# Fixed orders of the first part drawn anew on all engines, with a narrower product for the low part of v

## The chip, the cores and the metric

The kernel runs on one core of a Trainium2 chip, in one launch. The metric is device microseconds (us) of one execution, on that core; the time of a kernel is the median of its timed runs. Besides these runs there is one profiled execution, whose trace gives the start and the length of every instruction. The engines are called as in the profile: PE (matrix products), PEld (loading of the stationary operand for PE), DVE, ACT and POOL (three engines for element-wise work) and SP (which issues the transfers, DMA).

## What is computed

The reference is a block of a transformer on one sequence of 2048 tokens with 576 features, all in float32:

```python
mod = (silu(c) @ w_mod).reshape(1, 6, 1, 576)          # sa, ca, ga, sb, cb, gb
h = layernorm(x) * (1 + ca) + sa
q, k, v = split(h @ wqkv)                              # 32 heads of 18 features
pq, pk = phi(q), phi(k)                                # phi(t) = t + 1 if t > 0 else exp(t), + 1e-6
kv = einsum("bhsd,bhse->bhde", pk, v)                  # state sums, over all tokens
z  = einsum("bhsd->bhd", pk)
o  = einsum("bhqd,bhde->bhqe", pq, kv) / (einsum("bhqd,bhd->bhq", pq, z) + 1e-6)
x = x + ga * (o @ wo)
h = layernorm(x) * (1 + cb) + sb
x = x + gb * (silu(h @ w1) @ w2)                       # 576 -> 4608 -> 576
```

## The kernel before

**Numbers in two parts.** Products on PE are not taken in plain float32 but in a rounded form ("fp32r" in the profile). Each operand is split into a high part (the rounded value) and a low part (the rest, a subtraction on DVE or POOL, line 121). A product of two such operands is three matmuls on PE: high by high, high by low and low by high. Low by low is left out as too small to matter. `x_passes` (L222 to L226) records these three passes for most products of the first part.

**Stages.** The first part, some 370 us, computes attention token tile by token tile (16 tiles of 128 tokens). The modulation vectors are summed from `w_mod`, which is transferred in pieces (`raw`) and multiplied and added on DVE into `tmod` (`mod_piece`, L519). The same is done at the very start for the two vectors that the first layer norm needs (L360, L362, tile `hT`). For a group of tiles at a time, x is normalised (`layernorm`, L160 to L193, tile `xt`, in two forms: 576 columns, and a copy of the last 64), transposed on PE (L214) and multiplied with `wqkv` (L226, banks `psK`). `kv_mm` (L582 to L592) adds each tile's state sums: for each of five groups of heads it keeps a 128 by 128 piece of v stationary, once its high part (h = 0) and once its low part (h = 1), and moves the matching columns of k, 128 columns of the high part and 128 of the low part, 256 in all. So low by low is computed here, though it isn't needed: the bank `kvp` holds two halves of 128 columns for a group, which are added afterwards. These are 16 x 5 x 2 = 160 matmuls of 256 columns.

When the sums are complete, they are multiplied with `wo`, which turns the attention of a token into one product with a matrix `mpart`. Then each tile goes through `attn_step` (L1193): POOL multiplies q by z (`prod`, L1195), DVE sums it and takes the reciprocal (`q_norm`, L744 to L756), POOL multiplies q by it (`pn`, L752) and copies the last 64 columns once more (L754), PE transposes `pn` in five pieces of 128 columns (`q_transpose`, L811; only the fifth needs the copy), ACT and DVE split the result into high and low part (`qT`), and PE multiplies it with `mpart` (`attn_out`, L817). In between stand the layer norm and the transposes for the MLP (`xn`, `H`, `S`, `hT`) and the first products of the MLP, for the first group of its hidden columns: `mlp_up` (L885) and `down` (L896), whose results DVE adds to the accumulators (L901).

**The rest.** From about 370 us on, the MLP goes by units. A unit takes 256 of the hidden columns and half of the tokens, and computes the first product (`up`, L1323) and the second (`down`, L1396) by a scheme with seven products for two by two blocks instead of eight; the sums of blocks that the scheme needs are made ahead (L1136 to L1139), and the results are added on DVE (L1404). Two banks take the `down` products in turn, so a bank must be added up before PE may begin the next one in it. The names of the seven operands of the second product are ha, hb, hc, hd, he with a half (0 or 1).

**What sets the order.** From the third unit on, the order is that of the program text, on all engines (`manual_schedule`, L1554). For all that is ahead of it, tables of fixed numbers set the order (`ORDERS`, L55 to L105): `arrange` (L107 to L117) takes the instructions of an engine as a scheduler has laid them down and ties each to the one that the table puts before it, by a dependency that costs no wait on a semaphore. The tables have a row for each engine. DVE, ACT and POOL do their instructions strictly in this order: one that waits holds up all behind it.

Of the kernel before, what the change touches and what calls it, by code (L numbers as in the profile page):

```python
# [16 lines left out]
P = 128  # L17
# [5 lines left out]
def kernel(ctx: ExitStack, tc, A_x, A_wqkv, A_wo, B_x, B_w1, B_w2, c, w_mod, out):  # L23
# [28 lines left out]
    def f32(ap):  # L52
# [4 lines left out]
            0-105 114 106-108 115 109-113 116-2585  # L57
        """,
        "DVE": """
            2-3 1 0 4 6-7 11-12 8 5 13-14 18 15 9 16 10 17 19-24 29 25 28 26-27 30-31 43-44 33-34 36-37 35 38 32 39  # L60
            41 40 45 42 47 46 50 48-49 62-63 51 64 52 65-66 57 87 67 58 53 59 56 84-85 60 80 86 88 55 83 81 68-69 82
            70-72 122 73 54 74 61 89 75-76 123 78-79 91 77 90 92 124 93-94 96-97 125 98 126 100 127 99 95 103 101
            104-105 102 108 106-107 109-111 132-133 135 134 136 138-139 137 141-142 140 143-144 112-113 146-147 145
            114 148 117 115 149 118 116 119-121 128 131 129-130 150-151 224 222-223 225-226 152-154 157 155 158 156
            159 162 176 160-161 177-179 163 180 165 228 164 181 227 166-167 169-170 168 171-173 193-194 196 195 197
            199 198 200 202 201 203-205 174 206 175 207 182 185 209 183 208 186 188 187 210 184 189 192 190 211 191
            212-213 216 214 217 215 218 220 219 221 229-230 232-233 231 234-237 240 238-239 241-243 246 244 247 245
            248-249 252 250-251 253-255 258 256-257 259 262 260-261 263 266 268 267 270 269 271 264-265 272-273
            275-277 281 274 279 282 280 278 283-285 288 286 289 303 295-296 290 306 302 307 291 314 292 315 297 323
            298-299 293 308 300 324 294 304 331 309-310 287 311 301 312 305 332 316 340 313 317-321 341 325 322 351  # L70
            326-329 333 352 362 334-336 330 337 363 343-344 338 370 345-346 339 347 349 342 348 371 380 350 353-361
            381 398 364-369 372 399 416 373-375 377 376 378 417 424 385 382 384 379 387-388 391-392 394 425 402 386
            389 403 390 404-406 393 407 413 383 408 397 395 409-411 396 414 418 415 412 419-422 400-401 423 426-428
            432 429 431 430 435 433-434 437-440 445 441 446 442 444 443 436 447-451 454 452-453 455 469 466 456 467
            463-464 457 468 458 471 459-460 475 477 484 462 483 472 465 461 478 473 485 474 470 486 480 479 495 487
            482 488 492 481 490 476 493 489 491 494 500-501 497 503 529 499 496 498 510-511 502 506 504-505 507-509
            523 515 512-514 518 528 516-517 527 519 521-522 520 524-526 531 530 533 532 534-535
        """,
        "Activation": """
            0-2 4-9 11 10 3 12 16 19 13 15 14 18 21 17 20 26-27 24 22 29 23 28 25 30-33 55 35 37 59 39 58 42 40 38  # L80
            43 36 41 44 56-57 50 53-54 51-52 45 34 60-61 46 48 47 49 62-63 65-67 64 69 68 70 72 71 73-75 77-78 76 79
            81 80 82-84 93 85 95 87 86 96 88 94 89-92 97 99 98 100-102 104-105 103 106 108 107 109 149 110-112 152
            150-151 153 113-114 116-117 115 118 120 119 121-122 131 123-124 133-134 132 126 125 127-130 135 137 136
            138-139 141-142 140 145 143 146 144 147-148 154-155 157-158 156 159 161 160 162-182 184 183 186 185 188
            187 189-191 193-195 192 196-198 200 202 199 201 203-208 217 212 209 214 213 210 216 219 211 215 224 234
            220 218 239 221-222 225 223 245 235 231-232 256 226 228 230 233 227 229 236 240 237-238 270 241 243 246
            248-250 242 244 247 272 251-254 257 255 278 266 260 262-263 267 265 268 259 269 271 264 258 261 293 273
            305 274-276 281 283 282 277 284 279 307 285-287 296 289 280 288 290 292 291 301-302 299 297-298 303 300
            304 306 294-295 308-311 313 312 315-316 314 322-323 317 320 318-319 321 344 341 324 338 325-326 343 342
            327 339 345 328 330 329 340 332 331 347 333-334 336-337 335 348-349 346 353 350 354-356 351-352 358 357  # L90
            359 387 365 364 363 368 360-362 369 371 374 370 372 366 376 367 373 378 375 377 384 389 379 385 381 380
            382-383 386 388 390-395 397 396
        """,
        "Pool": """
            3 6 0 4-5 2 7 9 8 10-15 20 16-17 19 18 21-26 34 28 27 31 29-30 35 32 38 36 42 33 37 45 39-40 48 43-44 51
            46 41 47 55 49-50 58 52-53 61 85 56 73 57 54 59 77 60 62-63 80 64 74 65 68 75 69 78 66 72 70 79 67 76 81
            71 82-84 95 90-93 86-88 94 101 89 103 105 99-100 97 106-107 121 98 96 102 123 104 108-111 124 114 125
            113 112 115 118 116 119-120 117 122 126-128
# [1493 lines left out]
```

## Time and profile before

| what | value |
|---|---|
| median of 3 runs | 1142.06 us (1140.82 to 1143.03) |
| profiled execution: time | 1139.88 us |
| profiled execution: span from first to last instruction | 1138.1 us |
| time around the span | 1.8 us |
| granted PE clock, mean over the span | 1.00 |
| PE busy | 1126.6 us, 7033 matmuls |
| DVE busy | 970.6 us |
| POOL busy | 649.4 us |
| ACT busy | 538.8 us |

The page gives busy times as shares of the span; matmuls overlap in the records, so a PE that is busy is not yet one that works at its peak rate. What a matmul costs in a row of others is therefore read from the distance of two starts, not from the duration of one. A row of a timeline has the start in us, the length in us, the engine, the line, the operation, result and operands by their names in the program, the shape and the count of instructions that the row groups; in brackets stands how long the engine stood idle before it, and what it waited for. A piece of a chain of waits has its start, its length and what it was.

### The profile page before, as it was taken

The numbers are of one execution on the slowest core, as the hardware profiler recorded it, in microseconds if no ns is written. First come the engines' busy times: TensorE is split into PE (matmuls) and PEld (weight loads), VectorE is DVE, ScalarE is ACT, GpSimd is POOL, SyncE is SP. The second block draws the span as 40 slices with busy tenths as digits, with TensorE's granted clock in tenths as the row PEclk, the third lists the DMA queues.
The fourth block names the chain that finished last, engine by engine and source line by source line (L and its number), as shares of the span: only waits on it lengthen the run. The fifth ranks groups of instructions, "written<-read, shape, count | busy, mean of one in ns | idle before, by whom it ended". The sixth has DMA issues, their size and how long they took to land.

```text
span 1138.1 us, 19287 instructions
## 1 busy us (share of the span) xinstructions
PE 1126.6 (99%) x7033; PEld 1041.0 (91%) x7033; DVE 970.6 (85%) x1543; ACT 538.8 (47%) x1112; POOL 649.4 (57%) x743
## 2 busy tenths in 40 slices
PE   8999999999999999999999999999999999999998
PEld 8999999999998889999999999999999999999998
DVE  7866743685879889999999999999999999999996
ACT  6643442547556544445444444454454444444441
POOL 2100000373715767766775777677767767776776
PEclk9999999999999999999999999999999999999999
DMA  9521100223359976977968779769678697697684
GB/s 281 198 84 33 42 7 1 71 84 115 141 194 340 350 262 252 359 270 267 346 262 330 300 257 350 273 255 363 265 284 332 265 342 285 256 344 275 258 306 156
DMA packets 58813, 269.03 MB, mean 236 GB/s; under 512 B 5724, under 2 KB 21856, under 8 KB 35680
## 3 DMA queue, kind: packets, MB, share of 16 engines
q1 hardware_dynamic: 58708, 267.80, 63.8%
q8 instruction: 56, 0.92, 0.3%
q14 instruction: 37, 0.30, 0.1%
q10 hardware_dynamic: 12, 0.00, 0.0%
HBM read 250.12 MB, written 16.78 MB: 235 GB/s over the span
## 4 chain that ended last, share of the span: by engine, by line
PE 93%; DVE 2%; DMA 1%; POOL 1%; ACT 1%; issue 0%; DVEq 0%; POOLq 0%
PE up L1323 34%; PE down L1396 32%; PE psK L226 12%; PE big L226 6%; PE big L896 2%; PE small L885 2%; PE kvp L588 2%; PE small L214 1%; DMA hT<-hd 1%; PE big L811 1%; PE psT L214 1%; PE kvp L412 1%; DMA raw<-in_w_mod_dram 1%; PE up L1426 1%; PE down L1426 1%; POOL prod L1195 0%
## 5 line engine op out<-in xcount | busy, mean ns | idle before, releaser
L1404 DVE TENSOR_TENSOR acc<-down,acc 128x576 f32<-128x576 f32 x330 | 246.2, 753 | 14.6 <-PE down L1396 5.3
L1323 PE MATMUL up<-hT,w 128*128 128x512 f32 x916 | 239.4, 390 | 0.1
L1323 PEld LDWEIGHTS up<-hT,w 128*128 128x128 f32 x916 | 164.5, 188 | 25.0 <-DMA hT<-hd 0.3
L1358 POOL TENSOR_TENSOR s<-f,f 128x256 f32<-128x256 f32 x66 | 51.6, 782 | 162.0 <-ACT f L1339 162.0
L1396 PE MATMUL down<-w,hb 128*128 128x288 f32 x792 | 120.6, 294 | 0.0
L1396 PE MATMUL down<-w,hc 128*128 128x288 f32 x792 | 120.6, 294 | 0.0
L1396 PEld LDWEIGHTS down<-w,hb 128*128 128x128 f32 x792 | 113.8, 188 | 5.1
L1396 PEld LDWEIGHTS down<-w,hc 128*128 128x128 f32 x792 | 113.7, 188 | 5.1
L121 DVE TENSOR_TENSOR w<-v,w 128x288 fp32r<-128x288 f32 (+1 forms) x170 | 114.4, 682 | 0.5 <-ACT w L1057 0.5
L1404 DVE TENSOR_TENSOR U<-down,U 128x576 f32<-128x576 f32 x132 | 99.5, 754 | 17.5 <-PE down L1396 15.6
L226 PE MATMUL psK<-w,hT 128*128 128x352 f32 (+3 forms) x506 | 106.2, 336 | 0.5 <-POOL w L317 0.5
L1323 PE MATMUL up<-room,w 128*128 128x512 f32 x348 | 91.0, 390 | 0.0
L1377 POOL TENSOR_TENSOR hc<-s,hc 128x512 fp32r<-128x512 f32 x66 | 89.4, 1354 | 0.0
L226 PEld LDWEIGHTS psK<-w,hT 128*128 128x128 f32 x506 | 82.0, 189 | 6.8 <-POOL w L317 0.7
L1339 ACT ACTIVATE f<-f 128x512 f32<-128x512 f32 x102 | 64.4, 631 | 48.9 <-DVE f L1344 26.5
L184 POOL TENSOR_TENSOR rstd<-ve,neghalf 128x4 f32<-128x4 f32 (+3 forms) x10 | 9.8, 977 | 134.5 <-DVE ve L183 134.4
L1342 DVE TENSOR_TENSOR f<-up,p 128x512 f32<-128x512 f32 x102 | 69.6, 683 | 12.8 <-PE up L1323 11.9
L1065 ACT CAST w<-v 128x288 fp32r<-128x288 f32 x85 | 36.7, 434 | 75.4 <-PE down L1396 65.9
L1362 POOL TENSOR_TENSOR f<-f,s 128x256 f32<-128x256 f32 x66 | 50.7, 769 | 36.3 <-DVE hb L1377 25.9
L1323 PEld LDWEIGHTS up<-room,w 128*128 128x128 f32 x348 | 62.5, 188 | 9.4
L1396 PE MATMUL down<-w,hd 128*128 128x288 f32 x396 | 63.0, 294 | 0.9 <-DVE acc L1404 0.9
L1396 PE MATMUL down<-w,ha 128*128 128x288 f32 x396 | 63.0, 294 | 0.0
(310 smaller groups left out, 2529.4 us busy)
## 6 DMA issues: line engine op xcount, KB each, us to landing
hT<-hd SPq DMA_DIRECT2D x66, 1280.0 KB, 5.9
hT<-hd SPq DMA_DIRECT2D x45, 1024.0 KB, 5.3
room<-hd SPq DMA_DIRECT2D x35, 1280.0 KB, 5.6
room<-hd SPq DMA_DIRECT2D x20, 1024.0 KB, 5.3
v<-in_B_w_dram SPq DMA_DIRECT2D x17, 576.0 KB, 6.7
v<-in_B_w_dram SPq DMA_DIRECT2D x17, 512.0 KB, 7.0
hd<-S SPq DMA_DIRECT2D x6, 1024.0 KB, 4.3
xt<-in_A_x_dram SPq DMA_DIRECT2D x16, 288.0 KB, 3.1
```

The source lines that it names most:

```text
L121: return V.tensor_sub(lo, full, f32(hi))
L214: T.transpose(ps[:, i * P : (i + 1) * P], xt[i][:, cidx * P : (cidx + 1) * P], ident)
L226: T.matmul(ps, xpart(a), wpart(b), start=n == 0, stop=n == len(XW) - 1)
L1065: A.copy(self.w2[n][:, 0], src)
L1323: T.matmul(ps, left, right, start=first and m == 0, stop=m == len(seq) - 1, skip_group_check=True)
L1339: A.activation(self.f[i, k], self.f[i, k], AF.Silu)
L1342: V.tensor_add(f, self.bank[bank[1]], self.p1)
L1358: G.tensor_add(self.s[:, 0:1], half(i, 0, 1), half(i, 1, 1))
L1362: G.tensor_sub(half(i, 1, 0), half(i, 1, 0), self.s[:, 1:2])
L1377: eng.tensor_sub(t[:, :, 1, :], src, f32(t[:, :, 0, :]))
L1396: T.matmul(ps[:, p, :HALF], self.a[i, n][:, u, p * P : (p + 1) * P], self.w.w2[n][:, v], start=n in (1, 5, 7, 6) and j == 0, stop=j == 2, ...
L1404: V.tensor_add(dst, ps[:, :, :HALF], dst)
```

## The change

Three things change. The tables in `ORDERS` are new for all five engines. `arrange` is called after the last unit instead of after the second, and PE's table reaches one product further, so that the last product of the second unit is placed by the table. And in `kv_mm` the low part of v moves only the high part of k, 128 columns instead of 256; the other 128 columns of its bank get nothing added.

```diff
     ORDERS = {
         "PE": """
-            0-105 114 106-108 115 109-113 116-2585
+            0-106 114 107-109 115 110-113 116-2586
         """,
...
         for j in range(NHC):
-            o = mod_ps(j)
+            o = mod_ps(j).rearrange("p (a q) -> p a q", a=2)
             for h in range(2):
+                n = 2 - h
                 T.matmul(
-                    o, vt[:, j, h, :], pkt[:, :, j * HG : j * HG + P],
+                    o[:, :n], vt[:, j, h, :], pkt[:, :n, j * HG : j * HG + P],
                     start=(t == 0 and h == 0 and j % 2 == 0), stop=(t == NT - 1 and h == 1),
                     skip_group_check=True,
                 )
...
         for u in units[:2]:
             do_unit(*u)
-    arrange()
     with tc.manual_schedule(engines=ENGINES):
         for u in units[2:]:
             do_unit(*u)
         for work, tokens in TAIL:
             unit.plain_down(work)
             run(tokens.split(), (unit, behind2), ())
+    arrange()
```

The number of instructions is the same on every engine (12201 in all, the same 6970 products on PE). Places change for some 316 instructions on DVE (98 by three places or more), 194 on ACT (52), 57 on POOL (14), 35 on SP (8) and 22 on PE; from the third unit on no engine's order differs. Line numbers of the changed kernel are one higher behind `kv_mm`.

On PE, at the end of the second unit, before (a row is the line, the operation, result and operands with buffer numbers, shape and count; `w25` is a piece of the second weight, `he1` an operand of the seven-product scheme):

```order
L1323 MATMUL up_4302<-hT_3823,wtb_3193 128x512 x2
L1396 MATMUL down_4506<-w21_4197,ha0_4366 128x288 x6
L1323 MATMUL up_4519<-hT_3605,w_3811 128x512 x6
L1396 MATMUL down_4458<-w23_4264,he1_4371 128x288 x6
L1396 MATMUL down_4507<-w27_4206,hd0_4387 128x288 x6
```

and with the change:

```order
L1324 MATMUL up_4302<-hT_3823,wtb_3193 128x512 x2
L1397 MATMUL down_4458<-w23_4264,he1_4371 128x288 x6
L1397 MATMUL down_4506<-w21_4197,ha0_4366 128x288 x6
L1324 MATMUL up_4519<-hT_3605,w_3811 128x512 x6
L1397 MATMUL down_4507<-w27_4206,hd0_4387 128x288 x6
```

The product of he1, the last of the second unit, has moved ahead of the first `down` product of the third unit (ha0) and of the `up` product behind it.

On POOL, where the attention of the tiles begins (some 228 us into the span), before (`prod` is q by z, `pn` the normalised q, and the copy is that of its last 64 columns):

```order
L754 COPY pn_2395<-pn_2395 128x64
L1195 TENSOR_TENSOR prod_2522<-acc1_96,z_94 128x576
L752 TENSOR_TENSOR pn_2453<-acc0_95,r_2457 128x576
L1195 TENSOR_TENSOR prod_2610<-acc1_96,z_94 128x576
L752 TENSOR_TENSOR pn_2524<-acc1_96,r_2528 128x576
L1195 TENSOR_TENSOR prod_2676<-acc1_96,z_94 128x576
L754 COPY pn_2453<-pn_2453 128x64
L754 COPY pn_2524<-pn_2524 128x64
```

and with the change:

```order
L1196 TENSOR_TENSOR prod_2522<-acc1_96,z_94 128x576
L755 COPY pn_2395<-pn_2395 128x64
L753 TENSOR_TENSOR pn_2453<-acc0_95,r_2457 128x576
L755 COPY pn_2453<-pn_2453 128x64
L1196 TENSOR_TENSOR prod_2610<-acc1_96,z_94 128x576
L753 TENSOR_TENSOR pn_2524<-acc1_96,r_2528 128x576
L1196 TENSOR_TENSOR prod_2676<-acc1_96,z_94 128x576
L755 COPY pn_2524<-pn_2524 128x64
```

The copy of pn_2453 now stands right behind the instruction that makes pn_2453, and no longer behind three others; the copy of pn_2395 has one `prod` ahead of it.

On DVE, some 352 us into the span, before (L901 adds a product of the MLP from a bank `big` to an accumulator, L121 takes a low part, L1137 is one of the sums of blocks, and hT_3823 the low part that an `up` product waits for):

```order
L901 TENSOR_TENSOR acc2_97<-big2_3875,acc2_97 128x576
L121 TENSOR_TENSOR S_3825<-S_3824,S_3825 128x512
L901 TENSOR_TENSOR acc2_97<-big1_3933,acc2_97 128x576
L121 TENSOR_TENSOR hT_3823<-sl_3897,hT_3823 64x512
L901 TENSOR_TENSOR acc2_97<-big0_3890,acc2_97 128x576
L1137 TENSOR_TENSOR S_3824<-S_3824 128x512
L121 TENSOR_TENSOR w_3811<-raw_3814,w_3811 128x256
L121 TENSOR_TENSOR hT_3823<-S_3824,hT_3823 128x512
```

and with the change:

```order
L902 TENSOR_TENSOR acc2_97<-big2_3875,acc2_97 128x576
L1138 TENSOR_TENSOR S_3824<-S_3824 128x512
L121 TENSOR_TENSOR hT_3823<-sl_3897,hT_3823 64x512
L121 TENSOR_TENSOR hT_3823<-S_3824,hT_3823 128x512
L121 TENSOR_TENSOR wtb_3193<-v_3812,wtb_3193 64x256
L121 TENSOR_TENSOR S_3825<-S_3824,S_3825 128x512
L1139 TENSOR_TENSOR S_3824<-S_3824,H_3606 128x512
L121 TENSOR_TENSOR S_3825<-S_3824,S_3825 128x512
L902 TENSOR_TENSOR acc2_97<-big1_3933,acc2_97 128x576
L902 TENSOR_TENSOR acc2_97<-big0_3890,acc2_97 128x576
```

The last row of before now stands fourth, with the sum that it needs right ahead of it, and the two additions from big1 and big0 have moved behind five others.

Two more places on DVE are told in words. In the first ten microseconds the table of before has L360 on `hT` ahead of L185 (`nm`), and two copies on `z` (L435) between the normalisations L193 that follow; the new one has the copies ahead of L183 (`ve`) and L360 behind the first normalisation. At 44 us the table of before has the addition L519 on `tmod` behind the first normalisation of a pair of tiles and three normalisations behind it; the new one has all four normalisations, and an addition L334, ahead of L519.

More of the change, by code (lines that the diff above doesn't have):

```diff
@@ L63 @@
[L63 to L67, printed above, removed]
@@ new lines @@
+            363 337 339 344 370 345-347 342-343 349 348 353 371 380 354-359 350 360 381 361 398 364-369 399 416
+            372-375 377 376 378 417 424 385 382 384 379 387-388 391-392 394 425 402 386 389 403 390 404-407 393 383
+            395 413 408 412 409 397 418 396 414 410 415 401 419 411 420-421 423 400 422 427-428 426 429 431-439 430
+            440 445 441 446 443 442 444 447-451 455 454 453 452 466 456 467 469 457 464 471 458-460 475 472 462 461
+            463 478 473 477 484 483 485-486 479 468 480 474 487 470 465 493 488 495 490 476 489 482 492 481 491 494
@@ new lines @@
+            39 56 40 38 42 41 44 43 58 45 50 53 59 54 34 51-52 60 46 48-49 47 61-62 65 63 66-67 69 68 70 64 71-75
+            77-78 76 79 81-82 80 83 93 95 94 84-85 96 87 86 88-91 97 92 99 98 100-102 104-105 103 106 108-109 107
+            150 149 110-111 151 112 153 152 113-114 116-117 115 118 120 119 121-122 131 133 123-124 132 134 126 125
+            127-130 135 137 136 138-139 141-142 140 145 143 146 144 147-148 154-155 157-158 156 159 161 160 162-182
+            184 186 185 183 188 187 189-190 193 191 194-195 192 196-198 200 202 199 201 203-208 212 217 209 214 213
```

61 lines of the change are left out of this document (28 added, 33 removed).

## The prediction

> **What bounds the kernel now.** First I read the page: the busy shares and the chain that ended last.
>
> ```profile
> span 1138.1 us, 19287 instructions
> PE 1126.6 (99%) x7033; PEld 1041.0 (91%) x7033; DVE 970.6 (85%) x1543; ACT 538.8 (47%) x1112; POOL 649.4 (57%) x743
> PE 93%; DVE 2%; DMA 1%; POOL 1%; ACT 1%; issue 0%; DVEq 0%; POOLq 0%
> ```
>
> PE is busy for 99% of the span and carries 93% of the chain. So a cut elsewhere gains only what PE waits for. Where PE waits shows in the busy times by stretch:
>
> ```profile
> 0.00:60.00 60.00, 55.60 (x390) 52.59 (x391) 47.90 (x107) 35.94 (x72) 9.80 (x17) 1.00 0.78 239
> 205.00:237.00 32.00, 30.59 (x225) 29.44 (x224) 22.94 (x35) 17.92 (x34) 19.06 (x19) 1.00 0.31 90
> 340.00:369.00 29.00, 27.95 (x171) 24.86 (x170) 26.92 (x41) 17.93 (x35) 15.01 (x15) 1.00 0.92 334
> 406.00:1138.00 732.00, 728.89 (x4372) 666.08 (x4370) 682.07 (x1006) 328.63 (x709) 524.19 (x608) 1.00 0.77 292
> ```
>
> The columns are the stretch, its length, then busy time of PE, PEld, DVE, ACT and POOL, the granted clock (1.00 everywhere) and the DMA share. PE lacks 4.4, 1.4 and 1.0 us in the first three; that, and the wait of term 1 below, is what new orders could take. The last stretch has the same order before and after, and PE is busy in 728.89 of 732 us, so I take a shift of its start to pass through to the end one to one.
>
> **The change part by part.** Six terms, each a place where PE waits or computes less. Negative is a gain.
>
> *1. The last product of the second unit (he1).* The timelines of PE and, in the fifth row, DVE:
>
> ```profile
> 401.61 0.96 PE L1396 MATMUL down<-w,ha 128*128 128x288 f32 x6
> 402.40 1.53 PE L1323 MATMUL up<-hT,w 128*128 128x512 f32 x6
> 403.77 0.96 PE L1396 MATMUL down<-w,he 128*128 128x288 f32 x6
> 405.68 1.04 PE L1396 MATMUL down<-w,hd 128*128 128x288 f32 x6 [0.94 <-DVE acc L1404]
> 404.77 0.76 DVE L1404 TENSOR_TENSOR acc<-down,acc 128x576 f32<-128x576 f32 x1 [2.16 <-PE down L1396]
> ```
>
> A group of six 288-column matmuls takes 402.40 - 401.61 = 0.79 us, so PE could have begun hd at 403.77 + 0.79 = 404.56, but began at 405.68: hd takes the bank that he filled, and DVE had to add it up first. PE lost 1.12 us. Now he stands where ha stood, 403.77 - 401.61 = 2.16 us earlier; DVE was idle for those 2.16 us and can add at 402.6, done by 403.4, over a microsecond ahead of hd. Next late would be ha, one place later; it takes the other bank, which was free at 401.61. **-1.1 us.** If the addition found DVE taken (two additions of 0.76 us ahead of it), 0.4 of this would go.
>
> *2. The copy of pn.* POOL, and in the last row PE:
>
> ```profile
> 229.97 1.17 POOL L752 TENSOR_TENSOR pn<-acc,r 128x576 f32<-128x576 f32 x1
> 231.10 2.42 POOL L1195 TENSOR_TENSOR prod<-acc,z 128x576 f32<-128x576 f32 x1
> 233.49 1.16 POOL L752 TENSOR_TENSOR pn<-acc,r 128x576 f32<-128x576 f32 x1
> 234.61 1.40 POOL L1195 TENSOR_TENSOR prod<-acc,z 128x576 f32<-128x576 f32 x1
> 235.96 0.40 POOL L754 COPY pn<-pn 128x64 f32<-128x64 f32 x2
> 234.67 0.60 PE L811 MATMUL big<-ident,pn 128*128 128x128 f32 x4
> 236.24 0.33 PE L811 MATMUL big<-ident,pn 128*128 128x128 f32 x1 [0.97 <-POOL pn L754]
> ```
>
> Four transposes ran at 234.67; the fifth, ready to follow 4 x 0.11 = 0.44 us later at 235.11, came at 236.24, 1.13 us late, because the copy of 0.2 us stood behind three long instructions. With the change it stands right behind the first row and is done at 231.4. What is late next is the conversion of the transposes' result on ACT and DVE, which followed in either case; I leave 0.1 us for it. The two instructions behind the copy start 0.2 us later, and PE takes the next pn only some 9 us on (the transposes at 244.03, quoted under 6). **-1.05 us.**
>
> *3. The low part of hT.* DVE, and in the last row PE:
>
> ```profile
> 353.61 0.76 DVE L901 TENSOR_TENSOR acc<-big,acc 128x576 f32<-128x576 f32 x1
> 354.39 0.82 DVE L121 TENSOR_TENSOR hT<-sl,hT 64x512 fp32r<-64x512 f32 x1
> 355.25 0.76 DVE L901 TENSOR_TENSOR acc<-big,acc 128x576 f32<-128x576 f32 x1
> 355.92 1.76 DVE L1137 TENSOR_TENSOR S<-S 128x512 f32<-128x512 f32 x1
> 357.60 0.41 DVE L121 TENSOR_TENSOR w<-raw,w 128x256 fp32r<-128x256 f32 x1
> 357.94 0.68 DVE L121 TENSOR_TENSOR hT<-S,hT 128x512 fp32r<-128x512 f32 x1
> 358.67 1.89 PE L885 MATMUL small<-hT,w 128*128 128x512 f32 x7 [0.55 <-DVE hT L121]
> ```
>
> PE waited 0.55 us idle (0.7 by start to start) for the low part that ended at 358.62. Two additions (1.5 us), a low part S (0.8) and a low part w (0.4) move behind it, 2.7 us in all, so it should be ready near 356, ahead of PE. **-0.7 us.** What is late next: DVE, now with more ahead of the low parts of hs for the `down` products that follow. In the row below the second of these was done at 364.50, and PE did not wait for it; how much there was to spare no row shows. One moved instruction of 0.7 us too many ahead of it costs between 0 and 0.7. I count **+0.4 us**.
>
> ```profile
> 363.82 0.68 DVE L121 TENSOR_TENSOR hs<-sl,hs 128x512 fp32r<-128x512 f32 x1
> ```
>
> *4. The normalisation at 49 us.* DVE, and in the last row PE:
>
> ```profile
> 46.35 1.42 DVE L519 SCALAR_TENSOR_TENSOR tmod<-raw,sc,tmod 128x1152 f32<-128x1152 f32 x1 [1.40 <-DMA raw<-in_w_mod_dram]
> 47.69 0.93 DVE L193 TENSOR_SCALAR xt<-xt,mv,rstd 128x64 f32<-128x64 f32 x2
> 49.20 0.57 DVE L193 TENSOR_SCALAR xt<-xt,mv,rstd 128x576 f32<-128x576 f32 x1
> 49.83 0.66 PE L214 MATMUL psT<-ident,xt 128*128 128x128 f32 x4 [0.35 <-DVE xt L193]
> ```
>
> L519 waited 1.40 us for a transfer with the normalisations behind it, and PE idled 0.35 us (0.5 by start to start). Now they run in that wait. The addition L519 itself ends later by the one or two of them that its wait doesn't hold, and PE takes its sums only in L526, far behind. The low parts of the next hT then stand behind two L519 and an L333, so I keep 0.1 of it back: **-0.4 us.**
>
> *5. The first twenty microseconds.* Single rows of DVE and, last, PE:
>
> ```profile
> 6.12 0.49 DVE L360 TENSOR_SCALAR hT<-hT,sc 128x512 f32<-128x512 f32 x1 [0.56 <-DMA hT<-in_w_mod_dram]
> 6.76 0.18 DVE L435 COPY z<-sc 64x64 f32<-64x64 f32 x1
> 7.19 0.19 DVE L435 COPY z<-sc 64x64 f32<-64x64 f32 x1
> 15.04 0.42 DVE L121 TENSOR_TENSOR hT<-raw,hT 128x256 fp32r<-128x256 f32 x1
> 17.23 1.55 PE L371 MATMUL kvp<-ones,hT 128*128 128x64 f32 x12 [0.24 <-DVE hT L362]
> ```
>
> Before, L360 ran while DVE waited for POOL's rstd. Now it stands behind `nm` and a normalisation, where nothing hides its 0.49 us; the two copies leave that chain (0.37 us), but stand ahead of `ve`, on which rstd waits, and cost some 0.2 there. That is +0.3 on the next L362. A few microseconds on, the low part of hT at 15.04 (0.42 us) moves ahead of the three L362 behind it. PE idles for the last of these at 17.23, so it pays: **+0.5 us**, between 0 (the copies' leaving pays for all) and +1.1 (nothing is hidden: 0.49 + 0.2 + 0.42).
>
> *6. The low part of v.* Eighty of the 160 matmuls of L588 go from 256 to 128 columns. Pieces of the chain of waits, unbroken runs of PE:
>
> ```profile
> 197.49 1.20 PE kvp L588 x10
> 244.03 0.55 PE big L811 x5
> 133.41 1.12 PE psK L526 x10
> 143.05 0.97 PE psK L533 x4
> ```
>
> 256 columns take 120 ns each (1.20 / 10). No fp32r matmul under 256 columns is in the trace. The nearest rows with 128 columns are the transposes, 110 ns, and one pass of the plain float32 product L526, 112 ns. By these the gain is 80 x 9 = **-0.7 us**. The low end: six 512 columns take 403.77 - 402.40 = 1.37 us, 228 ns each, and 288 columns 0.79 / 6 = 132, so a column costs 0.43 ns; 128 fewer are 55 ns, 80 x 55 = -4.4 us. The high end: a plain float32 product is two such passes, 2 x 112 = 224 ns for 128 columns; if the narrow form ran at that rate, it would cost 80 x (224 - 120) = +8.3 us. I take 110 ns, since two unlike operations of the same width agree on it.
>
> The Trainium skill ("TensorE: Matmul & The Clock Gate", LDWEIGHTS) gives the loading of a stationary operand as its columns over 1.2, 107 ns for 128 columns; the rows of 110 and 112 ns agree, and by it the gain would be at most 80 x 13 = 1.0 us. The same page (Back-to-back issue gap) gives a sustained 81 ns for a matmul of 128 columns, an estimated gain of 80 x 39 = 3.1 us; the rows at hand disagree.
>
> *The sum.* -1.1 - 1.05 - 0.7 + 0.4 - 0.4 + 0.5 - 0.7 = -3.05. For the other moves (98 on DVE by three or more places), whose covers are thin in the MLP's first products (DVE is busy in 26.92 of 29 us there), I keep 0.15 back: **-2.9 us**. The profiled execution, 1139.88 us (span and 1.8 us around it), becomes 1137.0. It lies 2.18 us below the median of the runs, and I take the same difference again: **1139.2 us** for the median.
>
> **The rivals.**
>
> *Narrow moves cost as plain float32 (slower).* Place: the 80 matmuls of term 6; price +8.3 us instead of -0.7. Against it: the program holds no second pass for them, PE has the same 6970 products. For it: no narrow one is in the trace, and every product of the first part that moves split data has 256 columns or more. It decides from 120 + 2200 / 80 = 148 ns on, where the -2.2 of the other terms is gone. Time: 1142.06 - 2.2 + 8.3 = 1148.2 us.
>
> *Narrow moves stream by the column (faster).* At 120 - 55 = 65 ns the time is 1142.06 - 2.2 - 4.4 = 1135.5 us. For it: from 288 to 512 columns the cost follows the columns. Against it: at 128 both rows above say 110.
>
> *The waits fill again.* DVE is near its limit around 350 us, and at the start the chain goes through DVE, POOL and ACT in turn. If terms 3 and 4 are lost to the next low part and term 5 costs its 1.1 us, what is left is -1.1 - 1.05 + 1.1 - 0.7 = -1.75 at best, and with one of the first two lost too about -0.7: 1140.3 to 1141.4 us.
>
> **How the numbers follow.** The forecast gets 0.53; its own range is 1138.0 to 1140.6 (term 5 from 0 to +1.1, and half a microsecond of terms 1 to 3). Narrow at plain rate 0.19, streaming by the column 0.08, waits filled again 0.16, and 0.04 for a new wait of more than 4 us on DVE, slower. A measurement of this kernel can tell about 0.2%, 2.3 us, from no change: the bounds are 1139.8 and 1144.3. Of the forecast 0.36 lies below 1139.8 and 0.17 above, so faster is 0.36 + 0.08 + 0.02 = 0.46, the same 0.17 + 0.14 = 0.31, slower 0.19 + 0.04 = 0.23. The range takes in both ends of term 6: from 1134.5 (streaming, with the 0.55 that terms 3 and the reserve hold back, and half of term 5 gained) to 1148.5 (the plain rate, with 0.3 of term 5).
>
> **What would show it.** Term 1: no idle time ahead of the group hd, and DVE's addition of he some 2 us ahead of it. Term 2: five transposes in one row near 233, no wait for POOL's copy. Term 3: no wait for hT near 358; a new one near 365 for hs. Term 4: no wait for xt near 49. Term 5: PE's group of twelve L371 begins 0.3 to 0.6 us later than 17.23. Term 6: ten matmuls of L589 in 1.15 us; 1.7 would be the plain rate, 0.9 streaming. The forecast is wrong if the row of term 6 reads otherwise, or if PE's idle time in the first 60 us grows by over 1 us.

## The result, and the profile after

The changed kernel takes 1138.23 us (median of 6 runs, 1137.4 to 1138.73); the kernel before, run beside it, 1141.53 us (6 runs, 1139.98 to 1143.03). The ratio is 0.9971 with a 95% interval of 0.9961 to 0.9981, so it is 0.29% faster, 3.3 us (2.2 to 4.5). The forecast was 2.9 us, and 1139.2 us for the median.

The two profiled executions are only 1.2 us apart: the span falls from 1138.1 to 1136.9 us. Why the timed runs show more is one of the questions below.

```profile
span 1136.9 us, 19287 instructions
PE 1126.8 (99%) x7033; PEld 1040.8 (92%) x7033; DVE 971.0 (85%) x1543; ACT 538.7 (47%) x1112; POOL 649.3 (57%) x743
```

The busy times have not moved; what matters is where PE stood idle. The same stretches of time as before:

```profile
0.00:60.00 60.00, 55.06 (x381) 51.93 (x382) 47.60 (x107) 35.69 (x71) 9.45 (x17) 1.00 0.80 238
...
205.00:237.00 32.00, 31.52 (x232) 30.40 (x231) 22.55 (x39) 18.18 (x34) 19.63 (x19) 1.00 0.33 92
...
340.00:369.00 29.00, 28.50 (x174) 25.53 (x173) 25.07 (x40) 17.83 (x35) 13.90 (x15) 1.00 0.97 352
```

PE now lacks 0.5 us instead of 1.4 between 205 and 237, and 0.5 instead of 1.0 between 340 and 369. In the first 60 us it lacks 4.9 instead of 4.4: this execution began worse.

**Term 1, he1.** PE's timeline where the second unit ends, and then DVE's addition:

```profile
401.26 0.95 PE L1397 MATMUL down<-w,he 128*128 128x288 f32 x6
402.05 0.96 PE L1397 MATMUL down<-w,ha 128*128 128x288 f32 x6
402.85 1.53 PE L1324 MATMUL up<-hT,w 128*128 128x512 f32 x6
404.22 0.96 PE L1397 MATMUL down<-w,hd 128*128 128x288 f32 x6
```

```profile
402.25 0.76 DVE L1405 TENSOR_TENSOR acc<-down,acc 128x576 f32<-128x576 f32 x1
```

The groups follow each other with no bracket of idle time, and DVE's addition of he is done at 403.01, 1.2 us ahead of hd.

**Term 2, the copy of pn.** POOL, and then PE:

```profile
229.56 1.19 POOL L753 TENSOR_TENSOR pn<-acc,r 128x576 f32<-128x576 f32 x1
230.81 1.45 POOL L755 COPY pn<-pn 128x64 f32<-128x64 f32 x1
```

```profile
235.46 0.71 PE L812 MATMUL big<-ident,pn 128*128 128x128 f32 x5
236.21 2.09 PE L226 MATMUL big<-w,qT 128*128 128x288 f32 x14
```

The copy comes right behind its pn (drawn out to 1.45 us here), and the five transposes run as one row of five, where four and one were before. The product behind them starts 0.75 us after the first transpose: 5 x 0.11 for the transposes and 0.2 us of waiting.

**Term 3, hT.** DVE, and then PE:

```profile
355.15 0.69 DVE L121 TENSOR_TENSOR hT<-S,hT 128x512 fp32r<-128x512 f32 x1
...
357.90 2.07 DVE L902 TENSOR_TENSOR acc<-big,acc 128x576 f32<-128x576 f32 x3
```

```profile
356.77 2.88 PE L886 MATMUL small<-hT,w 128*128 128x512 f32 x12
```

The low part is done at 355.84 instead of 358.62, the additions come behind it, and PE takes the twelve matmuls in one go that were five and seven with a wait between.

**Term 4, the normalisation at 49 us.** DVE, and then PE:

```profile
46.59 1.06 DVE L193 TENSOR_SCALAR xt<-xt,mv,rstd 128x576 f32<-128x576 f32 x2
49.31 1.42 DVE L519 SCALAR_TENSOR_TENSOR tmod<-raw,sc,tmod 128x1152 f32<-128x1152 f32 x1 [1.66 <-DMA raw<-in_w_mod_dram]
50.64 0.75 DVE L333 TENSOR_SCALAR acc<-psK 128x576 f32<-128x576 f32 x1
```

```profile
50.37 0.60 PE L214 MATMUL psT<-ident,xt 128*128 128x128 f32 x4
51.45 0.50 PE L226 MATMUL psK<-w,hT 128*128 128x512 f32 x1 [0.48 <-DVE acc L333]
```

The normalisations run ahead of the transfer as told, and PE no longer waits for xt. But L333, which empties a bank that PE needs next, stands behind L519, and L519 waits for the transfer. PE waits 0.48 us for that instead.

**Term 6, the narrow matmuls.** A piece of the chain of waits: ten in 1.09 to 1.11 us, before 1.19 to 1.21.

```profile
55.36 1.11 PE kvp L589 x10
```

**The lead of PE.** The table has the start of the same matmul in each trace, less its start in the trace of before (us; negative is earlier, positive is later), near the time of before at the head of a column; at 403 it is the last product ahead of the ones that change places. A gain or a loss is a step from one column to the next; what one row has all along is how the execution began. The kernels are those of the experiments below.

| kernel | 36 | 53 | 204 | 230 | 241 | 356 | 362 | 380 | 403 | 412 |
|---|---|---|---|---|---|---|---|---|---|---|
| changed kernel | 1.10 | 1.23 | 0.75 | 0.79 | -0.13 | -0.05 | -0.91 | -0.71 | -0.35 | -1.58 |
| orders_only | 0.80 | 1.10 | 1.38 | 1.37 | 0.42 | 0.44 | -0.41 | -0.30 | 0.06 | -1.16 |
| start_old | 1.34 | 0.63 | 0.42 | 0.46 | -0.47 | -0.33 | -1.19 | -0.91 | -0.54 | -1.68 |
| kv_equal | 1.04 | 0.41 | -0.47 | -0.44 | -1.38 | -1.37 | -2.22 | -1.98 | -1.60 | -2.74 |
| late_old | 0.35 | -0.02 | -0.83 | -0.79 | -1.75 | -1.72 | -2.58 | 0.55 | 0.55 | -0.64 |
| kv_only | 0.94 | 1.27 | 0.46 | 0.50 | 0.51 | 0.68 | 0.88 | 0.88 | 0.88 | 0.88 |
| he1_only | 0.93 | 0.39 | 0.59 | 0.58 | 0.60 | 0.72 | 1.08 | 1.08 | 1.08 | -0.10 |
| pn_only | 0.73 | 0.19 | 0.19 | 0.18 | -0.09 | 0.21 | 0.46 | 0.46 | 0.46 | 0.46 |
| pn_dve | 0.50 | 0.14 | 0.14 | 0.13 | -0.81 | -0.57 | -0.33 | -0.33 | -0.33 | -0.33 |
| hT_only | 0.41 | -0.15 | -0.15 | -0.16 | -0.13 | -0.15 | -1.01 | 10.14 | 10.13 | 10.13 |
| hT_sp | 1.40 | 1.96 | 2.16 | 2.14 | 2.16 | 2.30 | 1.45 | 2.95 | 2.95 | 2.92 |

The first row has the account of the change: 0.9 us at 235, 0.86 at 358, 1.23 at 404, 0.5 between 53 and 204, and 0.56 given back between 362 and 403. Behind 412 the lead stays at -1.58 us, until one late transfer takes 0.8 of it at 826 us:

```profile
826.48 1.65 PE L1324 MATMUL up<-hT,w 128*128 128x512 f32 x6 [0.50 <-DMA hT<-hd]
```

### The profile page after: what moved, and what is told of

Its sections match the earlier page's. It is cut to its first block, busy times and chain, and to the rows that moved or that the text cites. A ratio compares the mean times of both kernels' runs of the same rounds, so it can differ in the third digit from the quotient of the medians.

```text
span 1136.9 us, 19287 instructions
## 1 busy us (share of the span) xinstructions
PE 1126.8 (99%) x7033; PEld 1040.8 (92%) x7033; DVE 971.0 (85%) x1543; ACT 538.7 (47%) x1112; POOL 649.3 (57%) x743
## 4 chain that ended last, share of the span: by engine, by line
PE 94%; DMA 3%; DVE 1%; ACT 1%; POOL 0%; SPq 0%; issue 0%; POOLq 0%
PE up L1324 34%; PE down L1397 32%; PE psK L226 12%; PE big L226 7%; PE small L886 2%; PE big L897 2%; PE kvp L589 1%; DMA hT<-in_w_mod_dram 1%; PE big L812 1%; DMA raw<-in_w_mod_dram 1%; DMA hT<-hd 1%; PE small L214 1%; DMA xt<-in_A_x_dram 1%; PE up L1427 1%; PE down L1427 1%; PE psT L214 1%
## 5 line engine op out<-in xcount | busy, mean ns | idle before, releaser
L1405 DVE TENSOR_TENSOR acc<-down,acc 128x576 f32<-128x576 f32 x330 | 246.2, 754 | 13.2 <-PE down L1397 3.2
L121 DVE TENSOR_TENSOR w<-v,w 128x288 fp32r<-128x288 f32 (+1 forms) x170 | 114.8, 684 | 2.8 <-ACT w L1058 2.8
L1405 DVE TENSOR_TENSOR U<-down,U 128x576 f32<-128x576 f32 x132 | 99.6, 754 | 17.1 <-PE down L1397 15.2
L1397 PE MATMUL down<-w,he 128*128 128x288 f32 x396 | 63.0, 294 | 0.0
```

The costliest lines, as they stand in the source:

```text
L121: return V.tensor_sub(lo, full, f32(hi))
L1397: T.matmul(ps[:, p, :HALF], self.a[i, n][:, u, p * P : (p + 1) * P], self.w.w2[n][:, v], start=n in (1, 5, 7, 6) and j == 0, stop=j == 2, ...
L1405: V.tensor_add(dst, ps[:, :, :HALF], dst)
```

## The experiments

The theory is the account of the prediction: six separate terms, each one wait or one cost. The rivals are that the gain hangs on other pieces of the tables than the ones named, that the narrow matmuls cost something else than a weight load, and that what the traces show at the start is chance. Since the tables number the same instructions before and after, pieces of the one can be set into the other where both have placed the same set. Line numbers differ by a few between these kernels.

**kv_only: the narrow product alone.**

```diff
-                    o, vt[:, j, h, :], pkt[:, :, j * HG : j * HG + P],
+                    o[:, :n], vt[:, j, h, :], pkt[:, :n, j * HG : j * HG + P],
```

> The kernel before with the narrow product alone; all orders as before. Theory (weight loads set the pace: 110 ns for any matmul of 128 stationary columns, and the wide one of a pair also falls from 119 to 110, since the pair of 256 and 128 columns takes no more than two loads): runs of ten in 1.10 us instead of 1.20, 16 of them, so 1.5 us less, ratio 0.9987. My term on record: 0.7 us less (0.9994). Streaming by the column: 4.4 us less (0.9961). If DVE and not PE sets the pace in this stage, the gain turns into waits and the time stays the same.

Measured: 1140.64 us against 1141.14, ratio 0.9997 (0.9988 to 1.0006). The runs of ten fell by 0.08 to 0.11 us each, as the theory had it, but some half of that is paid back behind the run, where a product of 288 columns holds PE for some 185 ns instead of 132. From 53 to 204 us, over fifteen tiles, PE gained 0.81 us and not 1.5: 0.05 us a tile and some 0.9 in all. The term on record (0.7) was nearer than the 1.5 of this expectation, and streaming by the column (4.4) is out. This kernel still has the start of before, and its first state sums began late all the same. A row of its PE (it groups five wide and five narrow ones under the shape of the first), and the same row before:

```profile
37.33 1.35 PE L589 MATMUL kvp<-pk,vx 128*128 128x256 f32 x10
```

```profile
36.39 1.44 PE L588 MATMUL kvp<-pk,vx 128*128 128x256 f32 x10
```

**orders_only: the new orders, wide product.**

```diff
-                    o[:, :n], vt[:, j, h, :], pkt[:, :n, j * HG : j * HG + P],
+                    o, vt[:, j, h, :], pkt[:, :, j * HG : j * HG + P],
```

> The changed kernel with the wide product of before; all orders as changed. By the two traces, the new orders lose 1.1 us up to 36 us and 0.1 to 0.4 us more up to 135 us, and win 0.9 at 235, 0.3 to 0.7 around 358 and 1.2 at 404: 0 to -0.9 us in all, ratio 0.9992 to 1.0. By the timed runs of before and after (-3.3 us) less 1.5 us for the narrow product, they would win 1.8 us, ratio 0.9984. The first says that the timed difference is partly the spread of the kernel before.

Measured: median 1139.34 us of 12 runs, 1141.14 before, ratio 0.9997 (0.9982 to 1.0013), which says nothing by itself: seven of the times lie between 1137.4 and 1139.6 us, five between 1142.9 and 1145.9. No trace of one of the five was taken, and what made them longer stays open, so that the gain of the new orders alone is shown by the trace and not by time. The trace has the same steps as the changed kernel at 235, 358 and 404 us (0.95, 0.85 and 1.22).

**start_old: the orders of before up to 41 us.**

```diff
     "PE" 0 to 111, "DVE" 0 to 78, "Activation" 0 to 55, "Pool" 0 to 8, "SP" 0 to 41 of the table:
-            0 3 2 1 4 6-7 11 8 12-13 9-10 14-16 18 17 5 19-22 30 23-24 28-29 25-27 43 31 44 33-34 36 35 37-38 32 39
+            2-3 1 0 4 6-7 11-12 8 5 13-14 18 15 9 16 10 17 19-24 29 25 28 26-27 30-31 43-44 33-34 36-37 35 38 32 39
...
```

> The changed kernel with the orders of before up to some 41 us on all engines, and the new ones behind. Theory: the loss of 1.1 us in the first 36 us comes from the new order there, so this is 1.1 us faster than the changed kernel (some 0.9961 to 0.9963 of before by the timed runs), and PE begins the first group of state sums at 36.4 instead of 37.5. Rival: the loss was the chance of one execution (transfers landing late), then this one equals the changed kernel.

Measured: 1139.32 us (8 runs), ratio 0.9981 (0.9969 to 0.9994), no faster than the changed kernel. The rival holds: PE stood at +1.34 us at 36 us with the old start. Over all traces taken, the old start stands at 0 (the kernel before itself), 0.41, 0.50, 0.73, 0.93, 0.94, 1.34 and 1.40, the new one at 0.35, 0.61, 0.80, 1.04, 1.10 and 1.52. The means are 0.8 and 0.9: the new start costs nothing that shows, and the profiled execution of before had the best start of all. In the chain of the changed kernel the late piece is a transfer of x that landed at 21.65 us; in the chain of start_old it is one of `wqkv` that landed at 25.79, and in that of before no transfer of the first 37 us stands.

```profile
14.24 7.41 DMA xt<-in_A_x_dram
```

Behind its start this kernel shows a cost of the new orders near 118 us. DVE, and then PE:

```profile
114.29 2.87 DVE L522 SCALAR_TENSOR_TENSOR tmod<-raw,sc,tmod 128x1152 f32<-128x1152 f32 x2 [1.91 <-DMA raw<-in_w_mod_dram]
...
117.33 0.75 DVE L336 TENSOR_SCALAR acc<-psK 128x576 f32<-128x576 f32 x1
```

```profile
118.14 0.50 PE L229 MATMUL psK<-w,hT 128*128 128x512 f32 x1 [0.33 <-DVE acc L336]
```

In the trace of before L333 (L336 here) stands between these two additions to `tmod`, at 114.59 us, and is done before PE needs its bank. Behind both of them it is late when their transfer is.

**kv_equal: all state-sum matmuls at 128 columns.**

```diff
-                    o[:, :n], vt[:, j, h, :], pkt[:, :n, j * HG : j * HG + P],
+                    o[:, h : h + 1], vt[:, j, h, :], pkt[:, h : h + 1, j * HG : j * HG + P],
```

> The changed kernel with all 160 matmuls of the state sums at 128 columns: high by high and low by low. The products high by low and low by high are left out. Theory (weight loads set the pace): the runs of ten stay at 1.10 us and the time is that of the changed kernel, within 0.3 us. Streaming by the column (61 ns each, as the distance behind a narrow one in the changed kernel's trace might suggest): runs of ten in 0.65 us and 7 us less.

Measured: 1137.55 us (5 runs), ratio 0.9965 (0.9953 to 0.9976), within the scatter of the changed kernel. A piece of its chain:

```profile
197.22 1.06 PE kvp L588 x10
```

Taking 128 columns off the other eighty matmuls too moved ten of them from 1.10 to 1.06 us only. By their single starts the matmuls of such a run follow each other at 109 to 115 ns; the first, where nothing holds the run up, takes 56 to 61 ns, and the product of 288 columns behind the run takes 184 instead of 132. In the trace of before, plain float32 products of 64 columns (L371) follow each other at 112 ns like those of 128. So something other than the columns sets the pace, at some 110 ns a matmul. By the Trainium skill ("TensorE: Matmul & The Clock Gate", LDWEIGHTS), the load of 128 stationary columns takes 107 ns; the trace agrees to within some 5 ns. The same page of the Trainium skill (Back-to-back issue gap) gives a sustained 81 ns for a matmul of 128 columns; no run of matmuls here goes at that pace.

**he1_only: PE's new order alone.**

```diff
-            0-105 114 106-108 115 109-113 116-2585
+            0-106 114 107-109 115 110-113 116-2586
```

> The kernel before with PE's new order alone (he1 ahead of ha0, and ten transposes near 26 us in another order); the product stays 256 columns wide. Theory: the wait of 1.12 us ahead of hd is gone and nothing takes its place, so PE's lead over before grows by 1.1 us between 402 and 412 us. Rival: the wait only moves to the bank of the next product, and less than 0.5 us is gained. By time some 0.9990 of before, which these rounds alone can't tell from 1.

Measured: 1139.63 us against 1141.33, ratio 0.9989 (0.9980 to 0.9998), and a step of 1.18 us between 403 and 412 us. PE:

```profile
402.69 0.98 PE L1398 MATMUL down<-w,he 128*128 128x288 f32 x6
403.51 0.99 PE L1398 MATMUL down<-w,ha 128*128 128x288 f32 x6
404.33 1.53 PE L1325 MATMUL up<-hT,w 128*128 128x512 f32 x6
405.69 0.96 PE L1398 MATMUL down<-w,hd 128*128 128x288 f32 x6
```

Term 1 is shown by itself, by the trace and, narrowly, by time: the interval leaves out 1.

**pn_only: POOL's copies alone**, and **pn_dve: DVE and ACT there too.**

```diff
     "Pool" 31 to 37 of the table (both kernels):
-            30 35 32 38 36 42 33
+            35 30 32-33 38 36 42
     "DVE" 283 to 315 (pn_dve; "Activation" 209 to 224 likewise):
-            283-285 288 286 289 303 295-296 290 306 302 307 291 314 292 315 297 323 298-299 293 308 300 324 294 304
+            283-284 288 285 289 286 295-296 290 306 303 302 291 307 292 314 293 315 294 297 323 304 298-299 324 308
...
```

> The kernel before with POOL's new order between 228 and 236 us alone (the copies of pn beside the products that make them). Theory: the fifth transpose no longer waits, PE gains 0.9 to 1.05 us between 230 and 241 us. Rival: the gain needs the new orders of DVE and ACT there too; then PE waits for the conversion instead and gains under 0.5 us.

> The kernel before with the new orders of POOL, DVE and ACT between some 221 and 245 us. Theory: with DVE's low part of the transposes' result moved up as well, PE gains 0.9 us between 230 and 241 us, where POOL's order alone gained 0.27. Rival: the gain of the changed kernel there needs yet other pieces; then it stays near 0.3.

Measured for pn_only: ratio 0.9998 (0.9989 to 1.0007), and a step of 0.27 us only. PE, and then DVE:

```profile
234.85 0.71 PE L813 MATMUL big<-ident,pn 128*128 128x128 f32 x5
236.26 1.95 PE L228 MATMUL big<-w,qT 128*128 128x288 f32 x13 [0.70 <-DVE qT L123]
```

```profile
234.48 0.45 DVE L180 BATCH_NORM_STATS2 st<-acc 128x6 f32<-128x288 f32 x1
235.08 0.35 DVE L753 RECIPROCAL r<-den 128x32 f32<-128x32 f32 x1
235.35 0.76 DVE L123 TENSOR_TENSOR qT<-big,qT 128x640 fp32r<-128x640 f32 x1
```

The five transposes run as one row, POOL's copy is in time, and PE now waits for the low part of qT, which DVE begins at 235.35 behind other work. With DVE's and ACT's new orders as well (one profiled run, 1139.99 us), it begins at 234.63 and the step is 0.94 us:

```profile
234.80 0.71 PE L813 MATMUL big<-ident,pn 128*128 128x128 f32 x5
235.54 2.75 PE L228 MATMUL big<-w,qT 128*128 128x288 f32 x19
```

```profile
234.63 0.77 DVE L123 TENSOR_TENSOR qT<-big,qT 128x640 fp32r<-128x640 f32 x1
```

So two waits, for POOL's copy and for DVE's low part, ended within a microsecond of each other, and the trace of before named only the later one.

**hT_only: DVE, ACT and POOL from 330 to 370 us**, and **hT_sp: SP behind 338 us too.**

```diff
     "DVE" 447 to 493 of the table (both kernels; "Activation" 314 to 358 and "Pool" 85 to 99 likewise):
-            447-451 454 452-453 455 469 466 456 467 463-464 457 468 458 471 459-460 475 477 484 462 483 472 465 461
+            447-451 455 454 453 452 466 456 467 469 457 464 471 458-460 475 472 462 461 463 478 473 477 484 483
...
     "SP" from 101 on (hT_sp):
-            102 101 105 104 119 103 118 117 106-107 110 108 112 109 111 113-116 123 120-122
+            101-102 104 103 119 106-107 105 110 117 108 118 112 109 111 113-116 123 120-122
```

> The kernel before with the new orders of DVE, ACT and POOL between some 330 and 370 us alone. Theory: the wait for hT at 358 is gone (0.7 to 0.85 us by 362 us), and the 0.5 us that the changed kernel gives back between 362 and 403 us in small waits comes in part from the additions put off there: 0.2 us lost near 364 us. Rival: all of what is given back comes from the new orders behind 370 us; then nothing is lost near 364.

> The kernel before with the new orders of DVE, ACT, POOL and SP behind some 330 us (DVE, ACT and POOL to 370 us). Theory: the 6.8 us for which PE waited with the first three alone came from SP's old order, in which the store of S landed 11.4 us after its issue and held up ACT, and then DVE; with SP's new order PE waits under 1 us there. Rival: the store is late because DVE and ACT make S late, whatever SP does; then the wait stays.

Measured for hT_only: 1150.51 us, ratio 1.0083 (1.0067 to 1.0098). The wait for hT is gone (a step of 0.86 us to 362), and then PE waits 6.65 us. One row each of PE, DVE and ACT, and the transfer in the chain:

```profile
373.87 2.53 PE L898 MATMUL big<-w,hs 128*128 128x288 f32 x9 [6.65 <-DVE acc L903]
```

```profile
372.45 0.69 DVE L123 TENSOR_TENSOR S<-H,S 128x512 fp32r<-128x512 f32 x1 [7.00 <-ACT S L1085]
```

```profile
371.80 1.66 ACT L1085 CAST S<-H 128x512 fp32r<-128x512 f32 x3 [6.92 <-DMA hd<-S]
```

```profile
360.36 11.41 DMA hd<-S
```

PE waits for an addition, which stands on DVE behind a low part, for whose high part ACT waits, until the store that frees its buffer has landed, 11.4 us after its issue. Neither theory nor rival had this. The wait of 6.65 us is not the whole loss, which is 11.1 us from 362 to 380 us: from 369.1 to 379.4 us the trace shows the granted clock at half, and while it lasts products of 288 columns follow each other at 240 ns instead of 132, some 2.6 us in all. A piece of that stretch (the granted clock is the third number from the end):

```profile
374.00:376.00 2.00, 2.00 (x9) 2.00 (x10) 1.96 (x4) 0.00 (x0) 1.30 (x2) 0.50 0.94 387
```

With SP's new order too (one profiled run, 1142.61 us) this wait is gone: the step to 362 is 0.85 us, 0.2 are lost by 368, and then PE waits 1.0 us for DVE near 378, where the tables of before go on. The theory holds, by one profiled run: the store's place on SP was the missing piece.

**late_old: the orders of before behind 370 us.**

```diff
     "DVE" from 494 on ("Activation" from 359 and "Pool" from 100 likewise):
-            491 494 529 500-501 499 497 496 498 510 503 502 511 507 506 504-505 508 515 509 514 527 513 512 518 528
+            491 494 500-501 497 503 529 499 496 498 510-511 502 506 504-505 507-509 523 515 512-514 518 528 516-517
...
```

> The changed kernel with the orders of DVE, ACT and POOL of before behind some 370 us; PE's order stays new. If the small waits of the changed kernel at 382 and 388 us (0.3 us in all) come from the new orders there, they are gone and it is 0.3 us faster than the changed kernel, ratio to before 0.9968; if DVE is simply behind with its work since 350 us, they stay.

Measured: 1139.94 us, ratio 0.9985 (0.9976 to 0.9994): not faster. In place of the small waits PE has two long ones:

```profile
366.04 1.86 PE L900 MATMUL big<-w,hs 128*128 128x288 f32 x12 [1.33 <-DVE acc L905]
...
376.73 1.66 PE L1327 MATMUL up<-hT,w 128*128 128x512 f32 x6 [1.07 <-DVE f L1346]
```

What the changed kernel gives back at 382 and 388 us is therefore not mended by the old orders; the new ones belong together. In the places of its small waits the load of the next stationary operand is held up to 0.12 us behind the end of an addition L1405 on DVE (382.14 and 387.86). That points to PE waiting for DVE, which is late with its additions, but no run tests it.

**kv_spread and kv_spread2: the pairs set between other products.** A tile's five pairs are queued and put behind every fourth (kv_spread, tiles 1 to 14) or second step (kv_spread2, tiles 1 to 13) of the product that follows:

```diff
             for m, (ps, wpart) in enumerate(outs):
                 T.matmul(ps, xpart(a), wpart(b), start=n == 0, stop=n == len(XW) - 1)
+                if pairs and (n * len(outs) + m) % (2 * len(outs)) == 2 * len(outs) - 1:
+                    pairs.pop(0)()
...
+        if 0 < t < NT - 2:
+            pairs.extend(lambda j=j: pair(j) for j in range(NHC))
```

> The changed kernel, with the five pairs of state-sum matmuls of a tile (256 and 128 columns) no longer in one run but each behind four 288-column or 352-column products that follow (for 14 of the 16 tiles; the order of the other engines is the same). Theory (weight loads of 107 us/1000 each are done ahead as long as PE streams, so a narrow matmul costs only its columns where wide ones around it leave time for the loads): a tile's pairs cost 5 x (119 + 62) = 0.91 us instead of 1.10 and the 0.05 us that the product behind a run pays, so 14 x 0.24 = 3.3 us less than the changed kernel, ratio to before some 0.994. Rival (only the next load can be done ahead): each narrow one still holds PE for a load, and the time is that of the changed kernel within 0.5 us.

> As kv_spread, but each pair of the state sums (256 and 128 columns) stands behind every second product step that follows, and the tiles spread are 1 to 13, so that all pairs of a tile are done before its buffers are filled again. By the trace of kv_spread the product behind a narrow matmul pays some 53 ns, wherever the narrow one stands: 61 + 53 = 114 ns for each. Theory now (only the next stationary operand is loaded ahead): the time is that of the changed kernel, ratio to before 0.996 to 0.998. Rival (loads even out over several products): 13 x 0.24 = 3.1 us less, ratio some 0.9945.

In kv_spread the sums of tile 14 come after its buffers are filled anew, so it adds other values for that tile and PE waits there; its time (1151.68 us, ratio 1.0090, 1.0076 to 1.0104) says nothing on the question, the price of its pairs does. kv_spread2 has the right sums: 1142.92 us (12 runs), ratio 1.0021 (1.0007 to 1.0035), slower than the changed kernel. Its PE:

```profile
57.83 0.74 PE L228 MATMUL psK<-wq,hT 128*128 128x288 f32 x4
58.41 0.34 PE L594 MATMUL kvp<-pk,vx 128*128 128x256 f32 x2
58.59 0.74 PE L228 MATMUL psK<-wq,hT 128*128 128x288 f32 x4
59.17 0.34 PE L594 MATMUL kvp<-pk,vx 128*128 128x256 f32 x2
```

Four products and a pair take 0.76 us (58.59 - 57.83). Four products alone take 4 x 0.132 = 0.53, so the pair costs 0.23, as in a run. By the single starts the narrow matmul holds PE for 60 ns, and the product behind it for 184 ns instead of 132 (288 columns, 25 cases). The theory holds in its price: loads do not even out over several products, so there is no gain to be had this way. Its time is not the one that the theory gave (0.996 to 0.998 of before): PE waits for DVE and ACT, 3.0 us in five waits between 92 and 160 us, and the likely reason is that the order of PE no longer fits theirs.

## Why the prediction was right

The total came out at -3.3 us (2.2 to 4.5) where -2.9 was forecast. Point by point:

- **Term 1** (-1.1): 1.23 us in the changed kernel, 1.22 in orders_only, 1.18 by itself. Right in mechanism and size.
- **Term 2** (-1.05): 0.92 us in the changed kernel, 0.94 in pn_dve. The five transposes ran in one row, at 235.46; the 233 named as their place did not fit the 234.67 of the term's own row. The size was right, but not the reason given for leaving only 0.1 us for the conversion behind: with POOL's order alone 0.70 us of PE's time go to it. The new orders of DVE and ACT there, which the term did not speak of, had to bring 0.67 of the 0.94 us, so that the size came out in part by luck.
- **Term 3** (-0.7 + 0.4): 0.86 us gained by 362, 0.20 lost by 380. In four kernels with the old order there (kv_only, he1_only, pn_only, pn_dve) PE lost another 0.2 to 0.4 us against the trace of before in the same place, so against the usual execution the gain is some 1.1. The wait for hs that was priced at 0.4 is at most 0.2: two stops of PE of 0.1 us each, at 363.9 and 364.1 by its starts, lie where DVE finished the second hs (364.01).
- **Term 4** (-0.4): failed. The wait for xt went and one for the bank behind L333 came in its place, as the third rival (waits fill again) had it; from 36 to 53 us the changed kernel lost 0.13. How much is lost or won there hangs on when the transfer lands: from 36 to 53 us kernels of the old order moved by between -0.56 and +0.56 us against the trace of before, and those of the new by between -0.71 and +0.30, -0.2 in the mean for both. Where the transfer held L519 up for some 1.7 us or more, PE lost 0.8 and 0.9 us with the old order (kv_only, hT_sp) and 0.5 and 0.6 with the new one (the changed kernel, orders_only), so something may be gained when the transfer is late; four traces are too few to show it.
- **Term 5** (+0.5): not borne out. L360 did move behind the first normalisation, and the next L362 began at 8.19 us instead of 7.91, as told; PE's group L371 began at 17.72 instead of 17.23, and at 36 us PE was 1.1 us late, which looks like the upper end of the term. The traces with the old start lie in the same place: in start_old the same group is 1.2 us late.
- **Term 6** (-0.7): some 0.9 us (kv_only). In the changed kernel 0.5 is seen from 53 to 204 us, since 0.2 went lost near 134 us; orders_only and start_old lost 0.3 and 0.6 near 118, kv_equal and late_old nothing, and no kernel of the old order over 0.1, so this is a cost of the new orders in some executions. Near 118 it is the wait of term 4 again (the rows stand under start_old); the loss near 134 stays open. The price was right because the rows it was taken from go at the same pace as the narrow matmuls, some 110 ns, whatever the columns. The two rivals on this term (65 ns and 224 ns a matmul) are out.
- **The reserve** (0.15): the small waits between 380 and 403 us cost 0.36.

Terms 4 and 5 were both priced from waits that belonged to one execution; their errors, some 0.4 us each, had opposite signs and cancelled by luck. The range holds the measured median only near its lower end: by the terms that it names, the forecast's own range comes out at some 1138.2 to 1140.3 us rather than 1138.0 to 1140.6. The forecast took the profiled execution as an ordinary one that was only 2.2 us quicker than the median. In fact it had the best start of all the traces and short waits up to 403 us: kernels with the old order there stood 0.4 to 0.7 us further back at 403 than at 53 us, apart from the pieces they had changed. That is why the two traces differ by 1.2 us and the timed runs by 3.3: the lead won from 53 to 412 us is 2.8 us in the changed kernel, and the old order loses half a microsecond there more often than not.

The time behind 412 us adds scatter to both. Waits of PE for a stream from memory, in kv_only:

```profile
PE up L1324 <- DMA hT<-hd: 0.8, 2, 0.6
PE up L1324 <- DMA room<-hd: 0.3, 1, 0.3
```

The columns are the sum, the count and the longest. The changed kernel had one such wait behind 412 us, the trace of before none and this one three. The place near 826 us is the same in the changed kernel, kv_only and kv_spread2; the other traces have no such wait there.

## What to carry to other kernels

Before a wait in the trace is priced, ask whether it belongs to the program or to the execution: a wait for an instruction that stands behind others is there again every time, one that goes back to a transfer may be elsewhere next time. Where one instruction is moved out of a wait's way, look for the second wait that ends just ahead of it, on another engine, since the trace names only the last. And tables of order for several engines are one thing: a piece of them alone, SP's places included, can cost ten times what it gains. In hT_only the missing place on SP cost a long wait and, on top of it, ten microseconds of the clock at half.

## What the runs showed of the hardware

In a row of narrow matmuls, each with a new stationary operand of 128 columns, one takes 108 to 115 ns here, however few columns it moves (64 or 128): 80 narrowed matmuls gave 0.9 us and not the 4.4 of their columns. Where a narrow one stands between wide ones it takes 60 ns by the starts, but the next pays the rest, 184 ns instead of 132 for 288 columns. This fits a load of one operand done ahead, and not of several, although loads and products overlap throughout (PEld is busy for 92% of the span).

A long wait of PE can cost more than its length: during the 6.65 us of hT_only the granted clock fell to 0.50 and stayed there up to 379.4 us, 5.5 us behind the wait, and during 5.7 us of waiting in kv_spread it fell likewise and stayed so up to 212.0 us, 4.5 us behind it. The waits of up to 1.4 us in the other traces left it at 1.00.
